# Linear attention beside a long convolution: inputs transposed by DMA from DRAM, the skip as a diagonal matmul, four angle multiples, merged products

## The chip, the cores and the metric

The kernel runs on one core of a Trainium2 chip. The metric is the device time of one execution in microseconds (us). Most executions agree within a few tenths of a per cent to one per cent; a run over 1.5% above the fastest of the same kernel is called slow and takes part in no comparison. Each run of a changed kernel was timed beside runs of the kernel before on the same chip.

Engine names in the profile: PE is TensorE's matmul, PEld its weight load, DVE VectorE, ACT ScalarE, POOL GpSimd, SP SyncE (which here only issues DMAs). Idle time always means the span less the engine's busy time.

## The reference, cut to what matters

Two independent branches, with 2048 positions and 448 channels each; their outputs stand side by side.

```python
def _A_ref(x, wqkv, w_phi, wo):                   # Hedgehog linear attention, 16 heads of 28
    q, k, v = split(x @ wqkv)
    pq, pk = q @ w_phi, k @ w_phi                 # per head
    phi_q = concat(softmax(pq), softmax(-pq)); phi_k = concat(softmax(pk), softmax(-pk))
    kv = phi_k.T @ v;  z = phi_k.sum(over s)
    o = (phi_q @ kv) / ((phi_q . z) + 1e-6)
    return o @ wo

def _B_ref(u, A_re, A_im, B_re, B_im, C_re, C_im, log_dt, Dskip):   # S4-type state space, N = 256
    dt = exp(log_dt);  A, Bc, Cc = complex parameters
    K[d, l] = real(sum_n Cc * exp(dt * A * l) * dt * Bc)            # kernel of 2048 taps
    y = irfft(rfft(u, 4096) * rfft(K, 4096))[:2048]                 # causal convolution
    return y + u * Dskip
```

## The kernel before

The program is recorded as some 1,090 small operations and then issued in a tuned order. Three long lists at the end of the source fix that order (`ORDER`), the buffer slots (`SLOTS`) and which operations use their alternative engine (`OTHER`). Helpers record the operations, so that most instructions of an engine carry the line of a helper: in the kernel before L164 is VectorE's tensor_tensor, L192 ScalarE's activations, L203 the matmuls and L218 the DMAs. In the changed kernel these are L177, L211, L222 and L240; L236 is the transposing DMA, L203 and L204 the Ln and the Exp of a reciprocal, L214 the evictions.

The 224-channel quarters of the 896 state columns go through the same stages: angle and damping tables (Sin and Exp on ScalarE), powers and products (VectorE), kernel taps (TensorE). The key side, the query side and the convolutions are woven in between. The parts that the change touches:

```python
def recip(o, a):                                    # the softmax sums and the denominators
    prog.add("V", lambda: low(lambda: nc.vector.reciprocal(o, a)))

def load_x(i):                                      # plain loads of x, 512 rows each
    dma("S", XS[i], x2[512 * i:512 * i + 512, :].rearrange("(p t) d -> p t d", t=4))
wq3 = A_wqkv.rearrange("(j p) n -> p j n", p=112)   # 448 = 4 chunks of 112 rows
# ... cut ...
dma("S", Wqk, wq3[:, :, 0:2 * D_MODEL])
# ... cut ...
def flip_x(i):                                      # TensorE transposes x, VectorE copies it out
    for tp in range(2):
        p = bank16(*prog.take("P", 6 + tp), [112, 2, 4, 128])
        transposes([(p[:, k, j, :], XS[i][:, 2 * tp + k, 112 * j:112 * j + 112], ident) ...])
        vcopy(xT[:, :, c0:c0 + 256].rearrange("p j (k x) -> p k j x", k=2), p)

def fold_weights(which):                            # wT = transposed weights, then Wp = W @ w_phi
    # ... TensorE transposes of Wqk into wT, copied out by ScalarE ...
    for jp in range(2):
        mms([(psum[0:112, b[k], ...], wT[:, which, c, 112 * (2 * jp + k):...], BD[:, c, :], ...) ...])
        acopy(Wp[which][:, 2 * jp:2 * jp + 2, :], two(b, 112))

def key_side():                                     # eight pairs of 128-row blocks
    # ...
    mms(acc(psum[:, b4, 0:D_MODEL], [(xT[:, dj, ts_], Wp[1][:, dj, :]) for dj in range(4)]))
    mms(acc(psum[:, b5, 0:D_MODEL], [(xT[:, dj, ts_], WV[:, dj, :]) for dj in range(4)]))
    for s in range(2):
        af(EK[:, t, s, :], psum[:, b4, 0:D_MODEL], ACT.Exp, scale=1.0 - 2.0 * s)
    # ... sums bz over each head ...
    recip(rk.rearrange("p t s h -> p (t s h)"), psum[:, bz, 0:64])

# ... order of recording: the inverse table GI, 2 x 1 MB, after the kernel spectra
for r in range(2):
    dma("G", GI[:, r], GI_d[r])
```

The softmax here doesn't subtract the row's maximum and nothing guards it: scores larger than these inputs give would overflow.

## Time and profile before

| | before |
|---|---|
| time, median of 4 runs | 286.48 us (284.81 to 288.85) |
| profiled span, mean clock | 284.6 us, 0.97 |
| VectorE busy / idle | 255.6 / 29.0 us |
| ScalarE busy, table loads | 202.2 us, 11 |

Span = busy + idle of VectorE. The prediction below shows the page's first lines.

### The profile page before, as it was taken

What the parts mean: (1) busy time and instruction counts of PE and PEld (TensorE: products, weight loads), DVE (VectorE), ACT (ScalarE), POOL (GpSimd) and SP (SyncE); (2) the same over time, 40 slices, a digit from 0 to 9 for tenths busy, and PEclk for the clock granted to TensorE, in tenths of its full rate; (3) what the DMA queues carried; (4) which work ended last, traced back from release to release, by engine and by line L of the source; (5) the groups of instructions that cost most, each with busy time, mean ns of one, the idle gap of its engine ahead of it and who ended that gap; (6) DMA issues with size and microseconds to landing.
All of it is one profiled execution on the core that took longest, in us unless ns stands there. A gap on an engine that the chain in (4) does not pass through costs nothing.

```text
span 284.6 us, 8940 instructions
## 1 busy us (share of the span) xinstructions
PE 236.7 (83%) x3932; PEld 179.9 (63%) x3932; DVE 255.6 (90%) x285; ACT 202.2 (71%) x340; POOL 16.1 (6%) x32
## 2 busy tenths in 40 slices
PE   1149899999999999999288977896989789897884
PEld 1149565756556587746187435782577789896874
DVE  4497999999999999799999999997999999499990
ACT  3759998989769989997899886869376224524241
POOL 8012101200000000000000010000000100000000
PEclk9999999999999999999779999998999959999999
DMA  7999375675353432513062648187789384747043
GB/s 166 229 232 243 89 209 120 142 191 129 67 131 65 67 131 59 83 36 87 6 137 46 134 118 323 19 191 222 281 267 324 72 275 85 192 59 155 2 99 68
DMA packets 64071, 39.49 MB, mean 139 GB/s; under 512 B 46736, under 2 KB 59424, under 8 KB 63648
## 3 DMA queue, kind: packets, MB, share of 16 engines
q1 hardware_dynamic: 61024, 31.57, 46.6%
q0 software_dynamic: 3008, 7.34, 8.2%
q8 instruction: 31, 0.51, 0.8%
q14 instruction: 8, 0.07, 0.1%
HBM read 26.36 MB, written 8.85 MB: 124 GB/s over the span
## 4 chain that ended last, share of the span: by engine, by line
DVE 36%; PE 32%; DMA 15%; issue 7%; ACT 5%; SPq 3%; POOL 1%; DVEq 0%; POOLq 0%
DVE sbuf L164 33%; PE psum L203 31%; DMA sbuf<-SCd 7%; DMA sbuf<-in_A_x_dram 5%; ACT sbuf L192 3%; SPq L218 3%; ACT sbuf L195 2%; DMA SCd<-sbuf 1%; DVE sbuf L189 1%; DVE sbuf L176 1%; DMA out_dram<-sbuf 1%; DMA sbuf<-in_B_u_dram 1%; PE psum L213 1%; POOL sbuf L218 1%; ACT L192 0%
## 5 line engine op out<-in xcount | busy, mean ns | idle before, releaser
L203 PE MATMUL psum<-sbuf 128*16 128x48 bf16 (+10 forms) x3824 | 229.0, 256 | 36.0 <-DVE sbuf L164 10.5
L203 PEld LDWEIGHTS <-sbuf 128*16 128x16 bf16 (+4 forms) x3824 | 171.5, 109 | 91.1 <-issue 28.3
L164 DVE TENSOR_TENSOR sbuf<-sbuf 128x896 bf16<-128x896 bf16 (+13 forms) x220 | 217.2, 1033 | 10.4 <-PE psum L203 3.5
L195 ACT CAST sbuf<-psum 128x448 bf16<-128x448 f32 (+4 forms) x128 | 70.9, 605 | 55.7 <-PE psum L203 54.1
L192 ACT ACTIVATE sbuf<-psum 128x448 bf16<-128x448 f32 (+4 forms) x140 | 83.9, 668 | 9.9 <-PE psum L203 9.7
L192 ACT ACTIVATE sbuf<-psum,sbuf 128x896 bf16<-128x896 f32 (+3 forms) x28 | 21.9, 814 | 4.4 <-DVE sbuf L164 2.3
L195 DVE CAST sbuf<-psum 128x896 bf16<-128x896 f32 (+2 forms) x13 | 12.4, 974 | 7.7 <-ACT sbuf L192 5.7
L213 PE MATMUL psum<-sbuf 128*112 128x128 bf16 (+2 forms) x108 | 10.3, 259 | 8.2 <-DVE sbuf L164 7.0
L213 PEld LDWEIGHTS <-sbuf 128*112 128x112 bf16 (+2 forms) x108 | 9.1, 165 | 9.8 <-DMA sbuf<-in_A_x_dram 5.5
L192 ACT ACTIVATE sbuf<-sbuf 128x896 bf16<-128x896 bf16 (+3 forms) x13 | 11.8, 905 | 4.6 <-DVE sbuf L164 3.9
L192 ACT ACT_TABLE_LOAD x11 | 14.1, 1283 | 0.9 <-PEq L909 0.7
L218 POOL DMA_DIRECT2D sbuf<-const x4 | 2.2, 551 | 118.3 <-PE psum L203 118.1
L218 POOL DMA_DIRECT2D sbuf<-in_B_u_dram x8 | 6.5, 827 | 18.1 <-PE psum L213 17.8
L176 DVE TENSOR_SCALAR sbuf<-sbuf 128x896 bf16<-128x896 bf16 (+3 forms) x8 | 4.9, 609 | 1.7 <-ACT sbuf L192 1.5
L182 ACT COPY sbuf<-psum 128x128 f32<-128x128 f32 (+2 forms) x10 | 4.3, 427 | 2.6 <-PE psum L213 2.1
L218 POOL DMA_DIRECT2D sbuf<-SUd x4 | 2.1, 528 | 69.3 <-DVE sbuf L164 42.3
L164 DVE TENSOR_TENSOR sbuf<-psum,sbuf 128x128 f32<-128x128 f32 (+3 forms) x10 | 4.7, 492 | 0.5 <-ACT sbuf L182 0.4
L176 ACT ACTIVATE sbuf<-sbuf 128x448 bf16<-128x448 bf16 (+1 forms) x3 | 4.4, 1455 | 0.9 <-DVE sbuf L164 0.9
L189 DVE RECIPROCAL sbuf<-psum 128x64 bf16<-128x64 f32 x8 | 4.4, 550 | 0.1
L182 DVE COPY sbuf<-psum 112x1024 bf16<-112x1024 bf16 x6 | 4.1, 684 | 0.3 <-PE psum L213 0.2
L179 DVE SCALAR_TENSOR_TENSOR sbuf<-sbuf 128x64 f32<-128x64 f32 (+1 forms) x6 | 3.0, 505 | 0.0
L198 POOL MEMSET sbuf<- 128x32 bf16 (+3 forms) x6 | 1.4, 258 | 18.4 <-DVE sbuf L164 18.1
(17 smaller groups left out, 18.4 us busy)
## 6 DMA issues: line engine op xcount, KB each, us to landing
sbuf<-const SPq DMA_DIRECT2D x16, 384.0 KB, 4.9
SUd<-sbuf SPq DMA_DIRECT2D x8, 448.0 KB, 3.7
sbuf<-SCd SPq DMA_DIRECT2D x16, 224.0 KB
sbuf<-SUd POOLq DMA_DIRECT2D x4, 896.0 KB, 5.6
sbuf<-const POOLq DMA_DIRECT2D x2, 1024.0 KB, 7.4
sbuf<-in_A_x_dram SPq DMA_DIRECT2D x4, 448.0 KB, 15.0
out_dram<-sbuf SPq DMA_DIRECT2D x4, 448.0 KB, 3.2
sbuf<-in_B_u_dram SPq DMA_DIRECT2D x16, 112.0 KB, 3.1
```

The lines of the kernel that those rows point to most:

```text
L164: prog.add("V", lambda: nc.vector.tensor_tensor(out=o, in0=a, in1=b, op=op))
L176: prog.add("V", lambda: nc.vector.tensor_scalar_mul(o, a, s), lambda: nc.scalar.activation(o, a, ACT.Copy, scale=s))
L179: prog.add("V", lambda: nc.vector.scalar_tensor_tensor(out=o, in0=a, scalar=s, in1=b, op0=op0, op1=op1))
L182: prog.add("V", lambda: nc.vector.tensor_copy(o, a), lambda: nc.scalar.copy(o, a))
L189: prog.add("V", lambda: low(lambda: nc.vector.reciprocal(o, a)))
L192: prog.add("A", lambda: nc.scalar.activation(o, a, fn, **kw))
L195: prog.add("A", lambda: nc.scalar.copy(o, a), lambda: nc.vector.tensor_copy(o, a))
L198: prog.add("G", lambda: nc.gpsimd.memset(o, v))
L203: nc.tensor.matmul(o, lhsT=l, rhs=r, **kw)
L213: nc.tensor.transpose(o, i, idn)
L218: prog.add(eng, lambda: e.dma_start(out=o, in_=i))
```

## The change

Its intent is to take work from VectorE, the busiest engine, and from TensorE. x, the query and key weights and the rows of u for the skip arrive transposed by the DMA, which makes TensorE's transposes and the copies of their results unnecessary. The skip is accumulated as a matmul with a diagonal. The products of the convolution are merged into larger instructions. Eight angle multiples become four, the others being made by ScalarE's scale. To suit blocks of 128, the 448 contracted rows are cut as 3 x 128 + 64. Six of the twelve reciprocals go to ScalarE as exp(-ln a), and the whole order is a new one.

```diff
-    def recip(o, a):
-        prog.add("V", lambda: low(lambda: nc.vector.reciprocal(o, a)))
+    def recip(o, a, t):
+        def by_exp():
+            nc.scalar.activation(t, a, ACT.Ln)
+            nc.scalar.activation(o, t, ACT.Exp, scale=-1.0)
+        prog.kind[len(prog.ops)] = "L"
+        prog.add("V", lambda: low(lambda: nc.vector.reciprocal(o, a)), by_exp)
+    def flip(o, i):
+        prog.add("S", lambda: nc.sync.dma_start(out=o, in_=i, transpose=True))
     def load_x(i):
-        dma("S", XS[i], x2[512 * i:512 * i + 512, :].rearrange("(p t) d -> p t d", t=4))
+        at = slice(512 * i, 512 * i + 512)
+        flip(xT[:, 0:3, at], x2[i::4, 0:384])
+        flip(xT[:, 3, at], x2[i::4, 320:448])
+    def chunk(t, dj, *at):
+        v = t[64:128, 3] if dj == 3 else t[:, dj]
+        return v[(slice(None),) + at]
-    dma("S", Wqk, wq3[:, :, 0:2 * D_MODEL])
+    for which in (1, 0):
+        for c in range(4):
+            c0 = D_MODEL * which + 112 * c
+            flip(wT[:, which, c, :], A_wqkv[:, c0:c0 + 128])
     # ... flip_x and the transposes of fold_weights go ...
-                mms(acc(psum[:, b4, 0:D_MODEL], [(xT[:, dj, ts_], Wp[1][:, dj, :]) for dj in range(4)]))
+                mms(acc(psum[:, b4, 0:D_MODEL], [(chunk(xT, dj, ts_), chunk(Wp[1], dj)) for dj in range(4)]))
     # ... the same for WV and the query side; args: four angle multiples in place of 2 x 4 ...
-                                  for cp in range(2) for mt in range(4)] + [(ident, UD[:, b, r, jt, :])])
+                                  for cp in range(2) for mt in range(4)]
+                                 + [(UT[:, r, 512 * b + 128 * jt:512 * b + 128 * jt + 128], DGD[:, qt, :])])
     # ... conv: products and finish steps of both blocks merged in quarters 0 to 2 ...
-        prog.run(ORDER or list(range(len(prog.ops))))
+        prog.run(ORDER or list(range(len(prog.ops))),
+                 lambda: nc.scalar.activation(sb(212672, [128, 1], F32), bias_hp, ACT.Ln))
     # ... new ORDER, SLOTS, OTHER ...
```

The last lines add a one-column Ln ("warm") ahead of a stretch of exponentials that holds a reciprocal.

## The prediction

> **What bounds the kernel now.** I read the page's summary and slices first, then the table of stretches, then ScalarE's timeline, the groups by form and the transfers.
>
> ```profile
> PE 236.7 (83%) x3932; PEld 179.9 (63%) x3932; DVE 255.6 (90%) x285; ACT 202.2 (71%) x340; POOL 16.1 (6%) x32
> PE   1149899999999999999288977896989789897884
> ...
> DVE  4497999999999999799999999997999999499990
> ACT  3759998989769989997899886869376224524241
> ```
>
> VectorE is busy 255.6 of 284.6 us, so 29 us are idle: some 8 in the first 14 us, 6.9 after its last instruction (277.7) and the rest in waits of 1 to 4 us. It is the first bound. ScalarE's 71% misleads: its digits are 7 to 9 until slice 29 (206 us) and low only afterwards, so it has little to spare where the tables are made. The stretches say so in numbers (columns: stretch, length, busy PE, PEld, DVE, ACT, POOL, clock, DMA share, GB/s):
>
> ```profile
> 0.00:20.00 20.00, 4.67 (x48) 3.81 (x49) 12.24 (x15) 10.32 (x13) 7.46 (x16) 1.00 0.96 206
> 20.00:40.00 20.00, 18.21 (x207) 14.41 (x208) 17.73 (x21) 18.67 (x23) 2.96 (x4) 1.00 0.67 174
> 40.00:60.00 20.00, 20.00 (x173) 12.77 (x172) 19.52 (x24) 18.29 (x33) 2.47 (x6) 1.00 0.71 173
> 60.00:80.00 20.00, 19.40 (x178) 11.95 (x176) 19.66 (x15) 16.86 (x30) 0.00 (x0) 1.00 0.44 93
> 80.00:100.00 20.00, 19.32 (x187) 11.83 (x185) 19.76 (x24) 17.37 (x30) 0.00 (x0) 1.00 0.47 93
> 100.00:120.00 20.00, 19.59 (x535) 15.63 (x532) 17.20 (x27) 18.54 (x28) 0.00 (x0) 1.00 0.39 97
> ```
>
> From 20 to 120 us three engines are near full at once. ScalarE's timeline where the rotation sines of quarter 1 end:
>
> ```profile
> 112.34 1.28 ACT L192 ACT_TABLE_LOAD   x1
> 113.63 0.92 ACT L192 ACTIVATE sbuf<-psum 128x896 bf16<-128x896 f32 x1
> 114.44 1.00 ACT L192 ACTIVATE sbuf<-psum,sbuf 128x896 bf16<-128x896 f32 x1
> 115.46 1.28 ACT L192 ACT_TABLE_LOAD   x1
> ```
>
> These sines end at 115.4, and VectorE's first large product of that quarter (a 6720-column one of 3.65 us) starts at 119.9. So ScalarE has only some 4.5 us in hand there. The groups and transfers that price the change:
>
> ```profile
> L164 DVE TENSOR_TENSOR sbuf<-sbuf 128x3584 bf16<-128x3584 bf16 x35 | 70.2, 2021 | 0.8 <-ACT sbuf L195 0.3
> L164 DVE TENSOR_TENSOR sbuf<-sbuf 128x896 bf16<-128x896 bf16 x66 | 38.9, 622 | 1.0
> L189 DVE RECIPROCAL sbuf<-psum 128x64 bf16<-128x64 f32 x8 | 4.4, 550 | 0.1
> L192 ACT ACT_TABLE_LOAD x11 | 14.1, 1283 | 0.9 <-PEq L909 0.7
> sbuf<-sbuf SPq DMA_TRANSPOSE x8, 4.0
> ```
>
> **What the Trainium skill says.** (1) "ScalarE: Activation LUTs", "What ACT_TABLE_LOAD costs": about 1283 ns a load, plus about 1380 ns of drain. The trace has 1283 ns, but the load at 112.34 ends at 113.62 and the next activation starts at 113.63: no drain shows, so I price 1.28. (2) Same page, "Table sets: the hidden batching unit": one set serves both exp and ln. The trace before has no ln. The order of the changed program, however, shows one load ahead of every ln and another ahead of the exp after it, so the combined set is not what was built. (3) "DMA: Bandwidth & Descriptors", "Latency and other measured facts": DMA transpose runs at an effective 261 GB/s. A 448 KB transpose here lands in 4.0 us, of which 1.76 us would be bytes at that rate; the trace doesn't contradict it. It has none from DRAM. (4) "VectorE: DVE Perf Modes", "Why tensor_tensor can't do 2x_2P or 4x": bf16 products reach two elements a cycle. From 1792 columns (1090 ns) to 3584 (2021 ns) the slope is 0.52 ns a column, which agrees, with 160 ns fixed. Merging saves only that fixed part.
>
> **The change part by part.** The description leaves out one thing: the diff lets ScalarE make a reciprocal as ln and exp. Six of twelve go there, and two one-column warming lns are added.
>
> VectorE, in sums of means. Convolution per quarter before: four 3584 (8.08), eight 896 (4.98), one 1792 (1.09) = 14.15. After, in quarters 0 to 2: one of 7168 (estimate from the slope: 3.88), two 3584 (4.04), four 1792 (4.36) = 12.28; quarter 3 only drops the skip product. Saved 3 x 1.87 + 1.09 = 6.7. Six reciprocals x 0.55 = 3.3. Copies of transposed x and weights that vanish (six of 0.68, two of 0.62, two of 0.27) 5.9. Query-side small operations 0.6 and negations 0.3. Against it: four evictions of 1.08 that come from ScalarE (4.3) and the diagonal (0.5). Net 12.0. Neighbours overlap (the means sum to 270.2 for 255.6 busy, 51 ns each), and 35 instructions fewer give back 1.8: busy about **245.4**, 10 less.
>
> ScalarE. Four angle multiples instead of eight replace 896-wide activations by narrow ones: 32 of 224 columns more (24 x 0.39 + 8 x 0.47), 16 of 448 more (12 x 0.56 + 4 x 0.65), 16 of 896 fewer (12 x 0.95 + 4 x 1.03) = +7.0, or +3.9 after its overlap of 97 ns an instruction. Copies gone: -5.3. Lns and exps: +1.9. Table loads go from 11 to 24 in the built order: 13 x 1.28 = **+16.7**, 14 of the 24 being due to the lns. Busy about 202 + 17 = **219**.
>
> TensorE loses 160 matmuls: 96 transposes, and 64 of 224 columns for the arguments. It was saturated at 40 to 120 us, so this shortens waits there; I give it no more. DMA: transposes of x (2.1 MB), weights (0.9) and u (2.1) replace plain loads; at 0.11 us of SyncE a 128x128 block (1.54 us for 14 in the trace) they take some 17 us of its queue, spread out. Neutral.
>
> **Where the gain goes.** By itself 10 us less on VectorE would give about 275. But VectorE waits for ScalarE at each quarter. In the changed order the last sine of quarter 1 has 178 instructions and 15 loads before it: 131.8 us of means, less 178 x 0.097 = 114.6 busy. Before, ScalarE had been busy 98.4 us at the corresponding 118.4 us (81.5 up to 100, then 16.9), so idle 20. The change puts 16 us more work ahead of this point. Of the 20 idle, 8 to 9 are the start-up wait for inputs, which stays; a ScalarE that is always behind loses perhaps 4 to 9 of the rest. So quarter 1 can go on at 114.6 + 9 + 6 = about **130** (125 to 134). VectorE's own work ahead of that point is 110 us, with 13 idle: 123. It waits some 7 us.
>
> Next gate, the exponentials of quarter 2: ScalarE has 44 us more (158.8 in all), so 130 + 44 + 2 = **176**, against VectorE's 130 + 36 + 2 = 168: 8 more lost. Before, that stage started at 163.5 with its first product already done at 157. From there VectorE has 99 us left; with 7 of tail and 4 of waits the end is 176 + 110 = **286** (281 to 292). Quarter 3 (37 us more of ScalarE against 42 of VectorE) binds no longer. The measured time is about 2 us above the span (286.7 for 284.6): 288. The low end of my gates gives 282. I put the middle at 287.
>
> **Rivals.** (a) *VectorE stays the bound.* ScalarE's waits were mostly for a saturated TensorE (its largest wait, 54 us in all), which now has less to do; if they vanish, the loads fill idle time: 275 span, 277. Against it: the 16 us ahead of quarter 1 are as much as all idle time there, start-up included. (b) *ScalarE's loads also break the key-side pipeline*, where four reciprocals sit between exponentials for TensorE: each takes 3.0 us instead of 0.55, and TensorE stalls with them: 293 to 297. For it: all three engines are full there. Against it: two sets of buffers. (c) *The DRAM transposes are slow or queue on SyncE* ahead of the key-side transposes: up to 5 us. Against it: 1.5 us each in the queue, and DMA is less than half busy after 60 us. (d) *The tail*: merged products delay the first inverse transforms, so the end waits for TensorE; 2 to 3 us, as only the unmerged quarter 3 ends the run.
>
> **Range and chances.** Middle 287, 278 (mostly rival a) to 296 (mostly rival b). Over 2% faster means below 281.6: 0.24. Slower means above 293.1: 0.18. Within 2%: 0.58.
>
> **What would show it.** ACT_TABLE_LOAD x24 with some 31 us; ScalarE busy near 219 and its digits at 9 until about 200 us; VectorE busy near 245 with 12 us or more of new waits for ScalarE ahead of quarters 1 and 2; transposes landing within 5 us. I am wrong if VectorE's idle total stays near 29 us (rival a), if loads number far fewer, or if the waits are for DMA or TensorE.

## More of the kernel before

The matmuls of the kernel before with a 448- or 512-wide result and 112 contracted rows, from the groups by form (columns: line, engine, operation, shapes, count; busy us, mean ns of one; idle before them):

```profile
L203 PE MATMUL psum<-sbuf 112*128 112x448 bf16 x256 | 54.6, 360 | 2.4 <-DVE sbuf L164 2.1 <-ACT sbuf L195 0.3
L203 PE MATMUL psum<-sbuf 112*112 112x512 bf16 x64 | 16.1, 381 | 0.8 <-ACT sbuf L195 0.7
```

One of the 256 lasts 360 ns, but 256 of them keep TensorE busy for only 54.6 us, 213 ns each: they overlap one another. Next, SyncE's DMA issues in the timeline of the kernel before (start us, duration us); each holds the queue for a microsecond or so:

```profile
6.81 1.08 SPq L218 DMA_DIRECT2D sbuf<-in_A_x_dram  x1
9.21 1.69 SPq L218 DMA_DIRECT2D sbuf<-in_B_u_dram  x2
11.69 0.35 SPq L218 DMA_DIRECT2D sbuf<-const  x1
```

ScalarE's timeline of the kernel before shows the first exponentials of the key side, the end of the start-up:

```profile
40.54 1.42 ACT L192 ACTIVATE sbuf<-psum 128x448 bf16<-128x448 f32 x3
```

And its transfers in the first 40 us:

```profile
DMA packets 5663, 7.62 MB, mean 190 GB/s; under 512 B 2112, under 2 KB 4032, under 8 KB 5533
```

## The result, and the profile after

| | before | after |
|---|---|---|
| time, median of 4 runs each | 286.48 us | 299.44 us (297.29 to 307.36) |
| profiled span, mean clock | 284.6 us, 0.97 | 295.5 us, 0.952 |
| VectorE busy / idle | 255.6 / 29.0 us | 247.8 / 47.7 us |

The change made the kernel slower: the ratio of the fast runs is **1.0421** (95% interval 1.0286 to 1.0556). Ratios here are the mean time of one kernel's fast runs over the mean of the other's of the same rounds, so not quite the ratio of the medians; one of the four runs after, 307.36 us, was slow and is left out. The time lies above the predicted range of 278 to 296.

The granted clock fell too, from 0.97 to 0.952, but that is not the loss: the fastest kernel below (0.9824 of the kernel before) was profiled at 0.949.

VectorE did lose 7.8 us of work, but its idle time grew by 18.7 us, and 18.7 less 7.8 is the 10.9 us by which the span grew. The page after (busy time of each engine; then VectorE's and ScalarE's digits):

```profile
PE 232.7 (79%) x3772; PEld 164.7 (56%) x3772; DVE 247.8 (84%) x250; ACT 216.7 (73%) x395; POOL 16.2 (5%) x32
...
DVE  5585689987779798899969578799999999999990
ACT  3698379988998998999899559759999534432442
```

VectorE's digits are low in the first five slices (37 us) and are 7 and 8 where they were 9 before. The stretches after (columns as in the prediction):

```profile
20.00:40.00 20.00, 11.65 (x96) 6.94 (x96) 12.93 (x14) 12.18 (x18) 3.72 (x7) 1.00 1.34 153
40.00:60.00 20.00, 19.98 (x140) 9.54 (x139) 17.62 (x20) 18.70 (x35) 1.12 (x3) 1.00 0.86 167
60.00:80.00 20.00, 17.96 (x148) 8.86 (x145) 15.95 (x16) 17.45 (x33) 0.00 (x0) 1.00 0.70 134
...
100.00:120.00 20.00, 18.13 (x255) 11.23 (x254) 15.93 (x27) 18.66 (x36) 0.00 (x0) 1.00 0.22 62
```

Set against the prediction's table: from 20 to 40 us ScalarE was busy 12.18 us instead of 18.67, VectorE 12.93 instead of 17.73 and TensorE 11.65 instead of 18.21. The three had no inputs: TensorE's timeline there names waits of 4.71 us for the DFT table and 2.73 for the transposed weights. From 40 to 120 us VectorE loses another 1 to 4 us in each stretch. Four causes offered themselves in the trace.

**A, table loads.** The groups of ScalarE after:

```profile
L211 ACT ACT_TABLE_LOAD x10 | 12.8, 1283 | 0.9 <-PEq L965 0.7
L203 ACT ACT_TABLE_LOAD x6 | 7.7, 1283 | 0.6 <-PE psum L222 0.5
L204 ACT ACT_TABLE_LOAD x6 | 7.7, 1283 | 0.1
```

With two more for the warming, these are 24 loads, as predicted. ScalarE's timeline at one reciprocal shows the pattern, and VectorE's waits (us in total, times, longest us) who pays:

```profile
64.94 1.28 ACT L203 ACT_TABLE_LOAD   x1
66.24 0.22 ACT L203 ACTIVATE sbuf<-psum 128x64 f32<-128x64 f32 x1
66.48 1.28 ACT L204 ACT_TABLE_LOAD   x1
67.77 0.26 ACT L204 ACTIVATE sbuf<-sbuf 128x64 bf16<-128x64 f32 x1
```

```profile
DVE sbuf L177 <- ACT sbuf L204: 10.3, 5, 2.4
```

Half a microsecond of activations costs 3.1 us of ScalarE, and VectorE waits five times for the result.

**B, the transposes from DRAM.** SyncE's issues in the timeline after, where those of 6.81 to 11.69 us stood before:

```profile
8.41 14.54 SPq L236 DMA_TRANSPOSE sbuf<-in_A_x_dram  x1
...
23.62 7.75 SPq L236 DMA_TRANSPOSE sbuf<-in_A_wqkv_dram  x4
```

One issue holds SyncE's queue for 14.54 us, and four more for 7.75; the weights are behind it. The five other issues of x in the first 60 us took 1.44 to 2.70 us, so it is not the issue itself that is long. That the transfers ahead of it (parameters, u, the table) held it is argued from its place; the trace names no cause. A plain load can be held there too: in the correct kernel at the end, a plain load of 64 rows of the value weights, issued at 10.64 us behind u, the table, the key weights and x, took 5.83 us. The transfers of the first 40 us, and those of x in the first 60 (median us from issue to landing):

```profile
DMA packets 11013, 6.63 MB, mean 166 GB/s; under 512 B 8340, under 2 KB 9956, under 8 KB 10884
```

```profile
sbuf<-in_A_x_dram SPq DMA_TRANSPOSE x6, 12.9
```

Twice as many packets carried fewer bytes. The landing time alone is no difference: the plain loads of x in the kernel before, of 448 KB each, had a median of 15.0 us in their first 40 us. What differs is what stood still behind them. The first exponentials of the key side came at 44.13 us instead of 40.54, and ScalarE had been busy 24.0 us by 40 us instead of 29.0.

**C, the 64-row chunk.** TensorE's groups by form after:

```profile
L222 PE MATMUL psum<-sbuf 128*128 128x448 bf16 x224 | 51.0, 365 | 4.8 <-DMA sbuf<-const 4.7
...
L222 PE MATMUL psum<-sbuf 64*128 64x448 bf16 x32 | 11.5, 360 | 0.0
...
L222 PE MATMUL psum<-sbuf 64*112 64x512 bf16 x16 | 6.7, 420 | 0.0
...
L222 PEld LDWEIGHTS <-sbuf 64*128 64x128 bf16 x32 | 3.0, 92 | 11.9 <-issue 11.9
```

A 64-row matmul still lasts 360 ns. Its group's 11.5 us (32 x 360 ns) does not say that it overlaps nothing: these matmuls stand singly between others of another form, and what two forms share is counted in both groups. The start times of single instructions in the trace settle it (medians): two 128-row matmuls of 448 columns start 189 ns apart, a 64-row one starts 285 ns after the one before it, and the next one 293 ns after that. Two such steps take 0.2 us more than two of 189 ns; for 48 short matmuls that is 9.6 us. The weight loads of 64 rows tell the same: they come late, with 11.9 us of idle time before them, 372 ns each. With overlaps counted once, all matmuls of 448 or 512 columns kept TensorE busy for 96.2 us before and 104.8 us after: 8.6 us more.

**D, the inverse table.** In the timeline of TensorE after, one kernel build stops in its middle:

```profile
171.36 0.53 PE L222 MATMUL psum<-sbuf 128*16 128x48 bf16 x15 [4.83 <-issue]
```

It waited for nothing that the profile shows. The first megabyte of GI was issued at 158.75 us; before, both halves were issued at 168.57, past that stage.

Last, the gate that the prediction set at 130 us, the first 6720-column product of quarter 1. In VectorE's timelines, before and after:

```profile
121.26 3.65 DVE L164 TENSOR_TENSOR sbuf<-sbuf 128x6720 bf16<-128x6720 bf16 x1
```

```profile
134.03 3.65 DVE L177 TENSOR_TENSOR sbuf<-sbuf 128x6720 bf16<-128x6720 bf16 x1
```

(The prediction has 119.9 for the kernel before. That is the start of a row of the timeline in which two smaller products come first.)

### The profile page after: what moved, and what is told of

Read it like the earlier page. It is cut to its first block, busy times and chain, and to the rows that moved or that the text cites.

```text
span 295.5 us, 8611 instructions
## 1 busy us (share of the span) xinstructions
PE 232.7 (79%) x3772; PEld 164.7 (56%) x3772; DVE 247.8 (84%) x250; ACT 216.7 (73%) x395; POOL 16.2 (5%) x32
## 4 chain that ended last, share of the span: by engine, by line
PE 42%; DVE 18%; ACT 13%; SPq 11%; DMA 9%; issue 6%; DVEq 0%; ACTq 0%
PE psum L222 41%; DVE sbuf L177 18%; SPq L236 7%; ACT sbuf L214 4%; SPq L240 3%; ACT sbuf L211 3%; ACT L204 3%; ACT L203 3%; DMA sbuf<-KTd 3%; DMA sbuf<-in_A_wqkv_dram 2%; DMA sbuf<-SCd 2%; DMA KTd<-sbuf 1%; DMA SCd<-sbuf 1%; ACT sbuf L204 1%; ACT sbuf L195 1%
## 5 line engine op out<-in xcount | busy, mean ns | idle before, releaser
L222 PE MATMUL psum<-sbuf 128*16 128x48 bf16 (+10 forms) x3760 | 231.9, 258 | 55.9 <-DVE sbuf L177 21.9
L177 DVE TENSOR_TENSOR sbuf<-sbuf 128x1792 bf16<-128x1792 bf16 (+14 forms) x203 | 213.2, 1091 | 23.9 <-ACT sbuf L204 10.3
L222 PEld LDWEIGHTS <-sbuf 128*16 128x16 bf16 (+4 forms) x3760 | 163.9, 110 | 122.9 <-issue 77.2
L214 ACT CAST sbuf<-psum 128x448 bf16<-128x448 f32 (+4 forms) x124 | 66.9, 609 | 43.1 <-PE psum L222 35.3
L214 DVE CAST sbuf<-psum 128x896 bf16<-128x896 f32 (+2 forms) x17 | 17.0, 1006 | 10.6 <-PE psum L222 7.3
L211 ACT ACTIVATE sbuf<-psum,sbuf 128x224 bf16<-128x224 f32 (+3 forms) x36 | 23.0, 702 | 1.3 <-DVE sbuf L177 1.2
L211 ACT ACT_TABLE_LOAD x10 | 12.8, 1283 | 0.9 <-PEq L965 0.7
L203 ACT ACT_TABLE_LOAD x6 | 7.7, 1283 | 0.6 <-PE psum L222 0.5
L189 ACT ACTIVATE sbuf<-sbuf 128x896 bf16<-128x896 bf16 (+2 forms) x5 | 4.8, 953 | 4.2 <-DVE sbuf L177 4.2
L204 ACT ACT_TABLE_LOAD x6 | 7.7, 1283 | 0.1
L189 DVE TENSOR_SCALAR sbuf<-sbuf 128x3584 bf16<-128x3584 bf16 (+3 forms) x6 | 5.0, 828 | 1.8 <-ACT sbuf L211 1.6
L177 DVE TENSOR_TENSOR sbuf<-psum,sbuf 128x896 bf16<-128x896 f32 (+2 forms) x6 | 3.5, 628 | 2.7 <-ACT sbuf L211 2.6
L195 ACT COPY sbuf<-sbuf 128x448 bf16<-128x448 bf16 (+1 forms) x6 | 3.0, 495 | 0.0
```

The source lines that it names most:

```text
L177: prog.add("V", lambda: nc.vector.tensor_tensor(out=o, in0=a, in1=b, op=op))
L189: prog.add("V", lambda: nc.vector.tensor_scalar_mul(o, a, s), lambda: nc.scalar.activation(o, a, ACT.Copy, scale=s))
L195: prog.add("V", lambda: nc.vector.tensor_copy(o, a), lambda: nc.scalar.copy(o, a))
L203: nc.scalar.activation(t, a, ACT.Ln)
L204: nc.scalar.activation(o, t, ACT.Exp, scale=-1.0)
L211: prog.add("A", lambda: nc.scalar.activation(o, a, fn, **kw))
```

## The experiments

Four theories, then, called A to D in the expectations. They predict different worths: if A is all, one table set gives back the whole loss; if B, the loss goes with plain loads whatever ScalarE does; C and D are small changes of shape and place. All ratios below are to the kernel before in the same rounds; the kernel after is 1.0421. "First exps" is the start of the key side's first exponentials.

**A: the reciprocals.** Two ways to take the loads away. First, all reciprocals back on VectorE (10 table loads):

```diff
-        prog.kind[len(prog.ops)] = "L"
-        prog.add("V", lambda: low(lambda: nc.vector.reciprocal(o, a)), by_exp)
+        on_v = lambda: low(lambda: nc.vector.reciprocal(o, a))
+        prog.add("V", on_v, on_v)
```

> The changed kernel with its six Ln/Exp reciprocals moved back to VectorE, so that 24 table loads become 10; nothing else differs. Theory A (the loads are what broke the key side and the query side): ScalarE falls by about 6 x 3.1 us of chain (14 loads of 1.28 us and 12 activations), to about 198 us; VectorE rises by about 4 us to 252; the waits of VectorE for the second activation of a reciprocal (10.3 us) go; the end comes 8 to 14 us earlier, about 285 to 290. Rival C (64-row matmuls saturate TensorE there) or B (start-up transposes): within 3 us of the changed kernel, 295 to 300, with the freed ScalarE time turning into waits for TensorE.

Measured: 292.0 us against 285.31, **1.0205** [1.0129, 1.0281]. Second, the reciprocals stay on ScalarE, but the set that holds both functions is loaded by name:

```diff
-                 lambda: nc.scalar.activation(sb(212672, [128, 1], F32), bias_hp, ACT.Ln))
+                 lambda: nc.scalar.preload_act_table_set("natural_log_exp_and_others"))
```

> The changed kernel with its reciprocals still on ScalarE, but with the table set that holds both Ln and Exp loaded by name ahead of the stage, so that 24 loads become 10 while the 12 Ln and Exp activations stay. If the loads are the cost in A, ScalarE falls by 14 x 1.28 = 18 us to about 199 and the end moves as far as with the reciprocals on VectorE, or 1 to 3 us further since VectorE keeps its relief. If it is the change of engines (two more hops per reciprocal) and not the loads, this run stays near the changed kernel while the one with reciprocals on VectorE gains.

Measured: 290.12 against 285.31, **1.0177** [1.0099, 1.0255], result correct. The page of this kernel:

```profile
PE 234.1 (81%) x3772; PEld 164.4 (57%) x3772; DVE 247.9 (86%) x250; ACT 200.2 (69%) x379; POOL 16.2 (6%) x32
```

10 loads remain and ScalarE is 16.5 us lighter, VectorE's idle time falls from 47.7 to 40.3. Both ways agree: A is worth 2.2 to 2.4%, some 7 us, a little less than the 8 to 14 us that were expected. It is not the whole loss, so the strict form of theory A falls. Whether the reciprocals stand on VectorE or on ScalarE makes no difference that shows; the loads do.

Two runs put the loads into the kernel *before*, which has none of B, C or D: the same recip, and six operations named in `OTHER`.

```diff
+    "250 265 280 310 450 630 "        # first try, temporaries at 187520 and 138528
+    "250 265 280 295 450 630 "        # second try, temporaries at 138272 and 138528
```

> Correct result. The kernel before with one part of the change alone: the corresponding six reciprocals as Ln and Exp on ScalarE, built as in the changed kernel with a separate table set for each (27 loads instead of 11, 16 x 1.28 = 20.5 us on ScalarE). Theory A, by itself sufficient: the key and query sides of the kernel before are as full as those of the changed kernel, so the end moves by as much as the loads moved it there or more, 7 to 12 us, 1.025 to 1.045. If the loads only hurt together with the other causes: within 1.5 per cent of the kernel before.

The first try missed: 320.57 us (1.1176), and infinities in the result. From the buffer map: the Ln's temporary overlapped the staging buffer of u's spectra before its DMA had read it, and one of the six stood among the sines, which forced extra set changes.

> Correct result. The kernel before with six reciprocals as Ln and Exp again, after the first attempt gave a wrong result (the Ln result's place was one that the spectra of u still held) and had one of the six in the middle of the sines: other places, and the fifth instead of the sixth pair of key blocks. 26 loads instead of 11. Theory A, sufficient by itself: at least 7 us slower, 1.025 or more; the first attempt, with its extra orders among engines, took 34 us. If the loads only hurt together with the other causes: within 1.5 per cent.

The second is correct: 312.69, **1.0931** [1.0847, 1.1015], with 26 loads. VectorE's waits:

```profile
DVE sbuf L177 <- ACT sbuf L204: 26.3, 6, 11.2
```

15 loads are 19 us, and the loss is 26: an order that was not made for these operations adds waits. So Ln and Exp with their loads do harm without B, C and D. How much of the 26 us is the loads and how much the move of the reciprocals to ScalarE is not shown (no run had one set in this kernel), and the size does not carry over to the kernel after, whose order was made with them.

**C alone, then with A.** The fourth chunk is contracted over all 128 rows, with zeros in the weights of rows 0 to 63 (they hold other, finite x):

```diff
-        v = t[64:128, 3] if dj == 3 else t[:, dj]
-        return v[(slice(None),) + at]
+        return t[:, dj][(slice(None),) + at]
+    # WV[0:64, 3] and Wp[which][0:64, 3] set to zero on GpSimd, one eviction of each Wp split in two, all on ScalarE
```

> The changed kernel with its fourth chunk contracted over all 128 rows, the 64 extra rows of the weights set to zero, so that no matmul of the key or query side has 64 rows. Theory C: the 48 weight loads' idle time of about 18 us falls and TensorE finishes the key side 6 to 9 us earlier; the end moves by 3 to 8 us, to 290 to 295. Theories A and B: TensorE only waits instead; within 2 us of the changed kernel, and the waits for ScalarE or the transposes grow.

On the kernel after: 299.05 against 285.31, 1.0482 [1.0404, 1.0561]. No gain.

> On top of the run with one table set: the fourth chunk contracts 128 rows, with zero weights in the first 64. In the run with one set TensorE was busy for the whole of 40 to 100 us, so if theory C holds (a 64-row matmul breaks the overlap with weight loads, about 9 us in all), the key side ends 5 to 8 us earlier and the end moves by 2 to 6 us, to 284 to 288. If C is wrong or VectorE or the start-up takes over: within 1.5 us of 290.

On top of one set: 292.89 against 285.76, 1.0238 [1.0169, 1.0307], no gain either against 1.0177 (the intervals overlap). Yet the edit did what it should inside TensorE:

```profile
L222 PE MATMUL psum<-sbuf 128*128 128x448 bf16 x256 | 55.5, 370 | 6.5 <-DMA sbuf<-const 5.7 <-DVE sbuf L206 0.8
```

No 64-row group is left. TensorE is busy 224.6 us, 9.5 less than with one set alone; its matmuls of 448 or 512 columns, overlaps counted once, take 97.2 us instead of 105.8. The cost of the short chunk is shown, but TensorE's spare time did not reach the end. The edit has a side effect: two evictions move from VectorE to ScalarE, so VectorE's work falls from 247.9 to 244.8 us, and what C does at the end can't be told from that.

**B: order of the queue, then plain loads.** First an attempt that leaves the transposes and moves u, the DFT table and the weights ahead of x (only the order of SyncE's issues changes: `32 33 38 19 20 21 18 40 39 7 6 12` in place of `7 32 33 38 6 40 19 20 21 18 39 12`).

> The changed kernel with the order of issue on SyncE altered in the first 30 us: the rows of u, the DFT table and the weights' transposes go ahead of both transposes of the first quarter of x. Theory B (a transpose that held the queue for 14.5 us delayed the table and the weights): the waits of TensorE for the table (4.7 us) and the weights (2.7 us) go, the first exponentials of the key side come at 40 to 41 us instead of 44.1, and the end comes 3 us or more earlier if that shift reaches the end, 0 to 1 us if later slack swallows it. A and C: end within 2 us of the changed kernel either way.

A miss: 298.1 against 285.31, 1.0459 [1.0383, 1.0535]. The hold only moved: in this kernel's (slow) profile four weight transposes held SyncE for 15.62 us from 7.11 on. Then all transposes of x and weights became plain loads of the same number of bytes, on top of one set. The result is wrong (relative error 0.59).

```diff
-        flip(xT[:, 0:3, at], x2[i::4, 0:384])
-        flip(xT[:, 3, at], x2[i::4, 320:448])
+        dma("S", xT[:, 0:3, at], rows_of(3))       # contiguous pieces of the same size
+        dma("S", xT[:, 3:4, at], rows_of(1))
-            flip(wT[:, which, c, :], A_wqkv[:, c0:c0 + 128])
+            dma("S", wT[:, which, c, :], A_wqkv[0:128, c0:c0 + D_MODEL])
```

> Result wrong on purpose. On top of the run with one table set: the 8 transposed loads of x and the 8 of the query and key weights become plain loads of the same number of bytes; everything after is the same. Theory B (the transposes occupy the queue of SyncE and the DMA engines and delay the first 40 us): no issue holds SyncE for more than 2 us, the DFT table lands before TensorE asks for it, the first exponentials of the key side come at 36 to 39 us instead of 42.6, and the end moves by 3 to 6 us, to 284 to 287. If later slack swallows it, within 1.5 us of 290.

286.85 against 285.76, **1.0036** [0.9967, 1.0106]: B is worth 1.4% by itself, though the intervals of the two kernels just overlap. First exps:

```profile
38.92 1.85 ACT L211 ACTIVATE sbuf<-psum 128x448 bf16<-128x448 f32 x4
```

That is 3.7 us earlier than the 42.58 of the one-set kernel, and earlier than in every kernel that keeps the start-up transposes. With C on top (wrong as well):

> Result wrong on purpose (plain loads). The run with one table set and plain loads (1.004 of the kernel before) plus 128-row contractions alone, without the later table load: it splits the last 2 per cent (about 6 us) of the three edits together between C and D. If the 64-row matmuls matter once the start-up is out of the way, 283 us or less (0.99 or less), and VectorE's idle time between 40 and 160 us falls from 11 to about 7 us. If it was the table load, 286 to 287 (1.00), and that idle time stays at 10 or 11 us.

285.39 against 287.56, 0.990 [0.9818, 0.9982]. C now seems to gain 1.4%, but the intervals overlap a little, and the profile is slow, so that the idle time named there can't be read.

**D: the table later**, on top of one set: half 0 of GI after u's spectra for the first convolution (178 us), half 1 on SyncE's queue after the kernel-spectrum tables.

```diff
-        dma("G", GI[:, r], GI_d[r])
+        dma("GS"[r], GI[:, r], GI_d[r])             # and both later in ORDER
```

> On top of the run with one table set (290.1 us, 1.018 of the kernel before): the inverse-transform table, 2 MB, is loaded later, its first half after the first load of spectra at about 178 us and its second half on SyncE after the kernel-spectrum tables at about 193 us, instead of the first half at 151.9 us. Theory D (this load fell on the score transfers of query block 2 and on TensorE's own instruction fetch): the 4.0 us stall of TensorE in the middle of a kernel build near 160 us falls to about 1 us, the 5.2 us that VectorE waits there for the scores falls to 1 or 2, and the end comes 3 to 6 us earlier, 284 to 287. Rival (the stall has nothing to do with that load): the stall stays at 3 to 5 us and the end within 1.5 us of 290.

290.5 against 285.76, 1.0167 [1.0102, 1.0232]: nothing at the end. The stall shrank as expected. One-set kernel:

```profile
163.89 0.52 PE L222 MATMUL psum<-sbuf 128*16 128x48 bf16 x15 [4.02 <-issue]
```

With the later table:

```profile
163.48 0.52 PE L222 MATMUL psum<-sbuf 128*16 128x48 bf16 x15 [1.57 <-issue]
```

VectorE's wait for the score transfers went from 5.2 to 3.65 us, too. The profiled runs differ elsewhere by as much: this one had 1.7 us more idle time at start-up. The other profiles agree in part. In the eight kernels with the early table this stop lasted 2.9 to 5.0 us, in the four with the later one and no transposes on TensorE 1.6 to 1.8, but in the five that transpose on TensorE 2.3 to 3.2, so the table is not its only cause. What ends such a stop can be read from the DMA records: in the traces TensorE stops 57 times for over 1 us with no wait, and each time it goes on 1.2 to 1.7 us after a 16 KB packet of the instruction queue has landed.

**All together.** A, C and D, with every transpose kept and the result correct:

> Correct result. The changed kernel with one table set, 128-row contractions and the later table load, all its DMA transposes kept. The same with plain loads took 0.982 of the kernel before. If the start-up transposes cost the 1.4 per cent that they cost without the other two edits, this comes to 0.995 to 1.003, 284 to 287 us; if they hide once TensorE has less to do, 0.982 to 0.99.

288.07 against 286.88, **1.0072** [1.0008, 1.0135], first exps at 45.59: above both expectations. And with B plain as well (wrong):

> Result wrong on purpose (plain loads). The three edits of this batch together on the run with one table set. If A, B, C and D explain the loss, the saving that was predicted for VectorE, some 8 us less work than the kernel before, now shows at the end: 272 to 280 us, 0.95 to 0.98 of the kernel before. If it stays at 284 or above, a further cause is missing.

281.05 against 285.76, **0.9824** [0.9766, 0.9881]: the kernel that was 4.2% slower is 1.8% faster than the one before, just short of the range expected. The order of the program is still the new one, so that order by itself is not the loss. Its page:

```profile
PE 225.3 (81%) x3772; PEld 170.0 (61%) x3772; DVE 245.2 (88%) x248; ACT 201.2 (72%) x383; POOL 17.7 (6%) x34
```

Between these two lies B alone, 2.5%, about 7 us. Which of the transposes? Only the later ones plain (x of the other three loads, query weights), the first x and the key weights transposed, on A, C and D (wrong):

> Result wrong on purpose. The run with one table set, 128-row contractions and the later table load (1.007), with only the later DRAM transposes, those of the last three quarters of x and of the query weights, turned into plain loads; the transposes of the first 32 us stay. With all of them plain it took 0.982. If the cost lies in the first 32 us: 1.00 to 1.01. If it lies in the later ones, which share the queue of SyncE with the transposes of the key exponentials: 0.982 to 0.99. In between: both.

288.33 against 286.6, 1.0051 [1.0012, 1.009]: no gain over 1.0072. SyncE still stands 15.51 us from 8.62, first exps at 45.85. As long as the transposes of the first 32 us stand, the later ones cost nothing that shows. That the first ones by themselves are all of B is not shown by this.

**A correct version.** So only x(0) and the key weights should go back to plain loads and TensorE. Three placements did not do it.

```diff
+        if i == 0:
+            dma("S", XS0, x2[0::4, :].rearrange("(k p) d -> p k d", p=128))
+            # and: dma("S", Wk, A_wqkv[:, D_MODEL:2 * D_MODEL].rearrange("(j p) n -> p j n", p=112))
+    # two transposes each on TensorE, copies to xT by VectorE and to wT by ScalarE
```

> Correct result. One table set, 128-row contractions, the later table load, and for the start-up only: the first quarter of x and the key weights loaded plainly and transposed by TensorE (16 + 16 transposes, two copies on VectorE and two on ScalarE) while the other three quarters of x, the query weights and u stay transposed by DMA. If theory B is right and the transposes under way in the first 32 us are the cost, this comes within 3 us of the wrong-result run with all three edits (281 us): 281 to 285 us, 0.98 to 0.995 of the kernel before, first key exponentials at 37 to 40 us. If the later transposes of x cost as much, or the added work delays the start-up, 286 to 289.

291.05 against 287.56, 1.0117 [1.0047, 1.0188]: the copies stood in ScalarE's path.

> Correct result. As the previous attempt with TensorE transposing the first quarter of x and the key weights, but with the transposes and their copies placed in gaps (ahead of and just after the sums of the kernel's zeroth row), since there the DFT of u and ScalarE waited for them by 3 and 6.6 us. Theory B: first key exponentials at 37 to 41 us and an end of 281 to 285 us, 0.983 to 0.995. If it is at 287 or more, the transposes of the rest of x, or the lost start-up time, are not cured this way.

286.85 against 286.88, 0.9996 [0.994, 1.0053]: TensorE waited 8.63 us for the key weights, which were queued behind the DFT table; first exps at 44.62.

> Correct result. As the last attempt with TensorE transposing the first quarter of x and the key weights, but with the weights' transposes after the DFT of u: there TensorE waited 8.6 us for the weights, whose load is queued behind the DFT table. Theory B: the first key exponentials come at 38 to 41 us instead of 44.6, and the end at 281 to 284 us, 0.98 to 0.99 of the kernel before, which is faster than both kernels. If it stays at 0.995 or more, what plain loads gain comes from the other three quarters of x and the query weights, not from the first 32 us.

285.62 against 286.95, 0.9972 [0.994, 1.0005], first exps at 43.19. By its expectation this spoke for the later transposes; the run with only these plain, above, spoke against them. Then key weights and x(0) were loaded behind the DFT table, and the transposes placed behind the first half of u's DFT, in psum banks 6, 7, 2 and 3:

> Correct result. The run with one table set, 128-row contractions and the later table load (1.007), with the first quarter of x and the key weights loaded plainly behind the DFT table and transposed by TensorE behind the first half of the DFT of u, so that neither u nor the table waits for them. The cost of the DRAM transposes lies in the first 32 us, so this should recover what plain loads recover, less the 32 matmuls and four copies: first key exponentials at 40 to 42 us (39 with plain loads, 43.2 in the third placement), end at 281 to 284 us, 0.98 to 0.99. At 0.995 or more the early start can't be bought back by TensorE's transposes in this order.

**284.55** against 286.72, **0.9938** [0.9898, 0.9978], correct, and 1.3% better than 1.0072: about half of what plain loads gain. Its page and its first exps:

```profile
PE 225.8 (80%) x3804; PEld 169.2 (60%) x3804; DVE 245.6 (87%) x250; ACT 202.9 (72%) x385; POOL 16.9 (6%) x34
```

```profile
41.75 1.85 ACT L211 ACTIVATE sbuf<-psum 128x448 bf16<-128x448 f32 x4
```

A variant with one of the two x copies on ScalarE (`(vcopy, acopy)[k2](...)`):

> Correct result. The same with one of the two copies of x on ScalarE instead of VectorE. If VectorE's chain of eviction and rotation powers near 30 us is what the copies delay, 0.5 to 1 us earlier than the other; if ScalarE is, as much later.

283.77 against 286.72, 0.9959 [0.9926, 0.9992], correct. The median is 0.8 us lower and the ratio 0.2% higher, so the question of this run stays open. Both beat both kernels, the one before by less than 2%, and they are the best of five placements. They keep the merged products, the diagonal skip, the four multiples and the later transposes.

VectorE's account over the kernels (idle by a time = time less busy up to it; us):

| kernel | ratio | busy | idle | of it by 40 us | by 120 us |
|---|---|---|---|---|---|
| before | 1 | 255.6 | 29.0 | 10.0 | 13.9 |
| after | 1.0421 | 247.8 | 47.7 | 13.6 | 26.8 |
| one set (A) | 1.0177 | 247.9 | 40.3 | 13.5 | 19.7 |
| A, C, D | 1.0072 | 245.4 | 43.9 | 15.6 | 23.6 |
| A, C, D, B plain (wrong result) | 0.9824 | 245.2 | 33.2 | 10.8 | 15.9 |
| A, C, D, first x and key weights on TensorE | 0.9938 | 245.6 | 36.4 | 12.3 | 19.0 |

(The profiled run of the fourth row took 291.29 us, above that kernel's median of 288.07. From the fourth row on some 2.5 us of VectorE's work are gone by the edit of C.) Down this list, A is worth 2.4%, C and D together 1%, and B 2.5%. The second figure is the least certain: the intervals of 1.0177 and 1.0072 overlap. The worths depend on the order in which the causes are taken out (B was 1.4% before C and D, 2.5% after).

## Why the prediction was wrong

**What held.** VectorE was priced at 245.4 us and measured 247.8. The 7168-column product was estimated at 3.88 us and took 3.887. ScalarE was priced at 219 and measured 216.7, with exactly 24 loads of 1283 ns. The mechanism "loads ahead of quarter 1 starve VectorE" was right: A alone moves the idle time by 120 us from 26.8 to 19.7. From the second gate on the sum held, too: that gate came at 187.3, and with the prediction's own 110 us behind it the end is 297, against a span of 295.5. Rival (a), that the loads fill idle time, is refuted: idle time went to 47.7 us, not 29. Rival (d) did not show: the tail stayed at some 7 us. One of the prediction's own signs of being wrong did: VectorE waited 10.3 us for ScalarE's reciprocals, but also 7.3 for TensorE and 6.3 for the score transfers. A small misreading is that ScalarE's digits before are "7 to 9" until slice 29: there are three 6s among them, and a 3 in that slice.

**The step that failed first: "DMA: ... Neutral", with "1.5 us each in the queue".** The 1.5 us were those of a free queue. Behind other transfers one issue held SyncE for 14.54 us, half of the first six x transposes needed 12.9 us or more to land (predicted within 5), and all that stood behind them in the queue was late: ScalarE had done 5 us less by 40 us. Rival (c) had it in words, at "up to 5 us" and with an argument against it that looks at the wrong stretch: "DMA is less than half busy after 60 us". The prediction's own table shows a DMA share of 0.96 in the first 20 us, where these transposes went. B measured 2.5%, some 7 us.

**The term of the gates that fell with it: "8 to 9 are the start-up wait for inputs, which stays".** It grew by those 5 us, so the sum 114.6 + 9 + 6 = 130 becomes 135; the first gate came at 134.03. The one-set kernel passed it at 129.04, the one with plain loads and A, C, D at 120.47. The second gate, VectorE's stage behind the exponentials of quarter 2, was put at 176 and came at 187.3: 11 us late after 4 at the first. In between VectorE stood 9.3 us: 2.4 for a reciprocal on ScalarE, 4.9 and 1.2 for the score transfers, the first of these beside the stop of TensorE (D), and 1.6 for the exponentials themselves. Which of these waits reached the end is not shown by a run.

**"TensorE loses 160 matmuls ... I give it no more".** It counted instructions and not shapes. Each 64-row matmul costs 0.2 us more than a 112-row one did, some 9 us in all, which took back most of what the dropped transposes gave (busy 232.7 for 236.7). That is shown inside TensorE. What it costs at the end is not settled: +0.6% with A alone, -1.4% where the start-up is cured, neither clear of its interval, and the edit also relieves VectorE.

**Rival (b), "two sets of buffers".** The buffers did not protect the key side: VectorE waited five times, 10.3 us in all, for a reciprocal on ScalarE. But this did not come on top of the middle. The middle had charged the loads with some 11 us (286 instead of 275); taken out of the kernel after, they give back some 7, their harm on the key side included. So the loads were not priced too low. What lay above the middle is what had been priced at nothing: B above all, with some 7 us, and C and D together with about 3, which is less certain. These worths do not add up exactly to the 12 us between 287 and 299.

**Where the expected gain went.** With 10 us less busy, 275 us of span needed idle time to stay at 29. The kernel with all four causes removed has 245.2 + 33.2 = 278.4, where 7.8 us of the lighter work are the change and about 2.6 the edit of C. The gain is there once nothing takes it, less the 4 us that its idle time is above 29. D is shown in part: most of the stop goes with the early table (4.02 to 1.57 us), and it ends after an instruction packet; how the table delays that packet is not shown, and nothing of it reached the end in the run that moved the table alone.

## What to carry to other kernels

Before moving loads to another kind of DMA, look at what the queue and the engines of DMA have to do in the same stretch and what is queued behind: start-up has no slack to hide it, and a transpose that TensorE does in an idle moment can be the cheaper one. Count table loads in the built order, and if two functions alternate, name the set that has both. Read the worth of a shape from start times or from the engine's total, not from the sums of groups. When the account is "busy time falls by 10 us", ask in the same breath for the idle time, and give each rival that hurts another stage a price of its own: here (c) was weighed as an alternative to the middle and came on top of it.

## What the Trainium skill lacked or had wrong

- "ScalarE: Activation LUTs", "Table sets: the hidden batching unit", counts an ln followed by an exp as one load, since one set has both. In this build every such pair took two (24 loads); loading that set by name brought it to 10 loads and 1.0421 to 1.0177. The page's rules do say to use that set; what they lack is that the loads which the build places alternate between two sets unless this one is loaded by name.
- "TensorE: Matmul & The Clock Gate", "Part 2: What happens when you issue a matmul", says that the row count does not matter for a weight load, and that loads are pulled ahead of running matmuls when row groups don't conflict or the load goes to the background buffer. The load times agree (92 ns with 64 rows, 102 with 128). But loads for 64 rows in rows 64 to 127, between 128-row matmuls, come late here: such a matmul starts 285 ns after the one before it and the next 293 ns after that, instead of 189 each. With 128 rows and zeros it came back (TensorE busy 9.5 us less). No run here tells 64 rows from the place of these rows.
- No page has it: transposing loads from DRAM behind other loads held SyncE's queue for 14.54 us in one issue (1.44 to 2.70 for the other five; 5.83 for a plain load at that place), and doubled the packets for fewer bytes (11,013 for 6.63 MB, 5,663 for 7.62 MB before).
- "Runtime: NRT & Kernel Launch", "Instruction fetch mechanics", has no size for a fetch that comes late. Here TensorE stopped for 4.0 to 4.8 us in the middle of a kernel build, with no wait in the profile, while a 1 MB table was being loaded, and for 1.57 us with the table issued later; all 57 such stops of over 1 us ended 1.2 to 1.7 us after a 16 KB instruction packet had landed.
